# Loads issued behind the key relay, attention scheduled piece by piece, and two pieces of preparation in another order

## The chip, the cores and the metric

One Trainium2 chip, one core of it. The time is the device time of one execution in microseconds (us), taken as the median of several runs.

## The reference

Gated linear attention with a complex decay, then a two-layer projection with a leaky relu. What matters of it:

```python
mag = np.sqrt(a_re * a_re + a_im * a_im)
scale = np.minimum(mag, 0.999) / (mag + 1e-06)
...
a_re_n, a_im_n = (a_re * scale, a_im * scale)
...
for t in range(S):
    ar, ai = (a_re_n[:, :, t, :, None], a_im_n[:, :, t, :, None])
    new_re = ar * S_re - ai * S_im
    new_im = ar * S_im + ai * S_re
    kv = np.einsum('bhd,bhe->bhde', k[:, :, t], v[:, :, t])
    S_re, S_im = (new_re + kv, new_im)
    y[:, :, t] = np.einsum('bhd,bhde->bhe', q[:, :, t], S_re)
```

In words (4 batches, 8 heads, 768 steps, 48 channels): each of 32 heads keeps a complex 48 x 48 state; at every one of 768 steps its rows are multiplied by the scaled decay, the product of k and v is added to the real part, and y is q times the real part. Then, with x the y of all heads side by side (3072 tokens x 384), w_in 384 x 2048 and w_out 2048 x 384:

```python
h = x @ w_in
g = np.maximum(0.01 * h, h)
return (g @ w_out).astype(np.float32)
```

## The kernel before

The sequence is cut in 6 chunks of 128 steps, and the work in 12 **passes** (`SUBS`), each one chunk of two of the four batches. A pass n has these parts:

- `fetch_a`, `fetch_qk`, `fetch_v` load the decay, q and k, and v by DMAs from SyncE's queue (SP).
- `prep(n)` on VectorE (DVE) and ScalarE (ACT) scales the decay, multiplies it up along the chunk (eight steps `r` by pairs of rows `u` and `a`, then over blocks by rows `xs`), spreads the block products again (`xt`, written into a part of tile `a`), forms the running decay in `a`, and multiplies q by it and k by its inverse into the tile `qkt`. Squares, logarithms and exponentials of this are ScalarE's (`sq`, `u1`, `w`).
- `relay_of(n, 0)` and `relay_of(n, 1)` move the q half and the k half of `qkt` to the tile `t96` (shown as `t`) by five DMAs each, so that channels of a head lie side by side. The second is called the key relay below.
- `attend(n)`: TensorE (PE) forms `scores` of four half batches; VectorE multiplies each by the mask (`asb`, in places the tiles `asd` and `more`); TensorE transposes the `keys`, which ScalarE copies to `kn` (`natural`); TensorE forms `values` into PSUM and the `update` of the state; ScalarE rounds the values to `xh` (`rounded`) and VectorE keeps the remainder `xl` (`rest`; both halves are one tile `x`); VectorE adds the update to the state `rst` (`summed_up`) and ScalarE multiplies it by the decay (`decayed`). In pass 0 keys and update come later (`late`).
- `forward()`: two passes' ends are one group g of 256 tokens. A group has eight stages s. `first(g, s)` forms `ph` by 18 matmuls (two halves of three k times hi·xh, hi·xl, lo·xh); `hide` makes `tg` (the relu) and splits it into `hid` high and low, on ScalarE and VectorE in turns; `second(g, s)` adds 18 matmuls into `po`. `store(g)` copies `po` to `ot` and writes it.

The weights arrive as 64-bit numbers. `convert(i)` splits them, in the first 81 us, into high and low parts `win_hi`, `win_lo`, `wout_hi`, `wout_lo`: two VectorE rows on a stage tile (`stage_st`, `stage_stg`, `stage_hid`...), one conversion on ScalarE, two matmuls with `idw` and `nid` into a bank of PSUM (`pd` or `att`), one copy back. `check_weights` reads the weights once more late in the run (`wck`, three ScalarE operations each), and `flag` sums up all checks by small operations on `scr` into `bad`, which decides whether a general version runs behind it.

All of this is given out by a list scheduler, `drive`. Each part is a generator that says before every step on which lane (engine) it goes, a "+" meaning that it needn't wait for the end of its last step, and which `Mark`s it needs. `drive` keeps a clock for each lane, advanced by the estimates `dve_cost`, `act_cost`, `pe_costs` and `dma_cost`, and takes the step that could start first; among those that could start within `look(rank)` after it, the one of lowest rank. `look` gives `SOON` for ranks between 0 and 200. The result is a fixed order for each engine; what really waits for what is then settled by semaphores. All instructions that go through a lane are issued in one helper and have its line, L121.

Of the kernel before, what the change touches and what calls it, by code (L numbers as in the profile page):

```python
# [13 lines left out]
AF = mybir.ActivationFunctionType  # L14
# [3 lines left out]
B, H, S, D = 4, 8, 768, 48  # L18
# [3 lines left out]
P = 128  # L22
# [6 lines left out]
TI = 3  # L29
# [46 lines left out]
PLACE = (8, 10, 11)  # L76
LATE = 1
LOOK = {R_RELAY: 0.2, R_ATT: 0.3, -1: 0.16}
SOON = 0.0


def look(rank):
# [93 lines left out]
def dma_cost(name, kw, aps):  # L176
    if name == "memset":
        return 0.3, 0.4
    out = kw["out"]
    if in_sbuf(kw["in_"]) and in_sbuf(out):  # L180
        each = out.nbytes() / 200e3
        return max(each, 0.6), each + 4.2
    each = out.nbytes() / 400e3
    return max(each, 0.6), each + 2.4

# [271 lines left out]
def body(ctx, tc, keep, a_in, qk_in, v_in, w_in, out):  # L457
# [111 lines left out]
    def attends_of(n):  # L569
        return [attended[n]]  # L570

    def fetch_a(n):
        yield "S", *([prepared[n - 2]] if n > 1 else freed(A) if n else []), *([loading[n - 1]] if n else [])
        N = TI * len(SUBS[n][1]) * C
        loading[n].set(0.0)
        raw_a[n] = a = a_0 if n == 0 else pp.tile([P, 3, N], F32, tag="a", name=f"a_{n}", bufs=2)
        spq.dma_start(
            out=a[:, 1:3], in_=a_in[a_off[n] : a_off[n + 1]].rearrange("(p l x) -> p l x", p=P, l=2)
        )

    def fetch_qk(n):
        yield "S", *([prepared[n - 1]] if n else [])
        N = TI * len(SUBS[n][1]) * C
        raw_qk[n] = qk = pp.tile([P, 2, N], F32, tag="qk", name=f"qk_{n}")
        spq.dma_start(
            out=qk, in_=qk_in[a_off[n] : a_off[n + 1]].rearrange("(p l x) -> p l x", p=P, l=2)
        )
# [24 lines left out]
    def freed(*places):  # L612
        return [x for x, r in zip(converted, ROUND) if r in places]
# [54 lines left out]

    carrying = {}

    def prep(n):
        yield "A", fetched_a[n], *([scaled[n - 1]] if n else []), *([spread[n - 2]] if n > 1 else [])
        c, bs = SUBS[n]
# [46 lines left out]
        yield "V"  # L720
        dve.tensor_tensor(out=a[:, 1:3, sl], in0=a[:, 1:3, sl], in1=two(s0), op=ALU.mult)
        yield "A"
        act.activation(a[:, 0, sl], a[:, 2, sl], AF.Copy, scale=-1.0)

        scaled[n].set(prepared[n].end + 1.0)
        pr = u1[:, 0 : 4 * M].rearrange("p (a b m) -> p a b m", a=2, b=2)
        for r in range(1, R):
            src = zr[:, :, r - 1]
            yield "V"
            dve.tensor_tensor(  # L730
                out=pr, in0=src.unsqueeze(2).to_broadcast([P, 2, 2, M]), in1=swap(ar, r), op=ALU.mult
            )
            yield "V"
            dve.tensor_tensor(out=zr[:, :, r], in0=pr[:, 0], in1=pr[:, 1], op=ALU.add)
# [27 lines left out]
            st *= 2  # L762

        xt = w1[:, 0 : 2 * M].rearrange("p (l x j) -> p l x j", l=2, j=J)
        for l in range(2):
            yield "+A" if l else "A"
            act.copy(
                xt[:, l].rearrange("p i (j x) -> p x j i", x=NB),
                xs[:, l, 0:J].rearrange("p (x j) i -> p x j i", x=NB),
            )  # L770

        def tj(ap, k):
            return ap.rearrange("p (r x j) -> p r x j", r=k, j=J)

        spread[n].set(prepared[n].end + 0.6)
        yield "V", *([moved_q[n - 1], moved_k[n - 1]] if n else freed(*QKT))
        qkt = pp.tile([P, 2, 2, TI, nb, TP], F32, tag="qkt", name=f"qkt_{n}")
        tb = qkt[:, :, 1].rearrange("p l i b t -> p l (i b t)")[:, :, :N]

# [135 lines left out]
    def attend(n):  # L915
# [24 lines left out]
        def masked_out(bi, hh):  # L940
            name = f"asb_{n}_{bi}_{hh}"
            if bi == 0:
                asb = pp.tile([P, 4, C], F32, tag="asb", name=name, bufs=2)
            elif not once:
                asb = pp.tile([P, 4, C], F32, tag="tg", name=name, bufs=2)
            elif hh:
                asb = pp.tile([P, 4, C], F32, tag="asd", name=name)
            else:
                asb = more[0][:, 2 * DM : 2 * DM + 4 * C].rearrange("p (h t) -> p h t", h=4)
            dve.tensor_tensor(out=asb, in0=ps[bi, hh], in1=mask, op=ALU.mult)  # L950
            am[bi, hh] = asb
            banks.give(ps.pop((bi, hh)), attended[n].end + 0.8)

        def keys(bi, hh):
            t96 = relay[n][1]
            ps[bi, hh] = bank = banks.take()
            for h4 in range(4):
                pe.transpose(
                    out=bank[:, h4, 0:96],
                    in_=t96[:, slot_of(1, hh * 4 + h4), bi, 0:C],  # L960
                    identity=ident[0:96, 0:96],
                )
# [47 lines left out]
        def rounded(bi):  # L1010
            xh, _, x0 = xgroup(u0 + bi)
            act.activation(
                xh[:, :, x0 : x0 + C], px[bi][:, 0:TI], AF.Copy, scale=XSC,
                accum_out=xacc[:, u0 + bi : u0 + bi + 1],
            )
# [34 lines left out]
                banks.give(pu.pop(bi), attended[n].end + 2.5)  # L1050

        yield "P", moved_q[n], moved_k[n], *at[0], *(attends_of(n - 1) if n else [masked]), banks.some(4 if once else 1)
        for k, (bi, hh) in enumerate(halves):
            if k and not once:
                yield "+P", banks
            scores(bi, hh)
        for k, (bi, hh) in enumerate(halves):
            yield "+V" if k else "V"
            masked_out(bi, hh)
        if carry and not late:  # L1060
            for bi in range(nb):
                yield "+P" if bi else "P", banks.some(2), *at[1]
                for hh in range(2):
                    keys(bi, hh)
                for hh in range(2):
                    yield "+A" if hh else "A"
                    natural(bi, hh)
        yield "P", fetched_v[n], banks.some(2 if late or not carry else 4), *at[2], *(
            [summed[g - 2]] if g > 1 else freed((X0, X1)[g])
        )  # L1070
        for bi in range(nb):
            px[bi] = banks.take()
            if carry and not late:
                pu[bi] = banks.take()
        for bi in range(nb):
            if bi:
                yield "+P"
            values(bi)
            if carry and not late:
                update(bi)  # L1080
            yield "A"
            rounded(bi)
        for bi in range(nb):
            yield "+V" if bi else "V"
            rest(bi)
        if not carry:
            return
# [26 lines left out]
    def first(g, s):  # L1114
        xh, xl, _ = xgroup(g * GT // C)
        shown[g, s] = ph = psh.tile([P, NF, GT], F32, tag="h", name=f"ph_{g}_{s}")
        for x in range(NF):
            if x:
                yield "+P"
            fs = slice((s * NF + x) * P, (s * NF + x + 1) * P)  # L1120
            for k in range(TI):
                mm(ph[:, x], lhsT=win_hi[:, k, fs], rhs=xh[:, k], start=(k == 0), stop=False)
                mm(ph[:, x], lhsT=win_hi[:, k, fs], rhs=xl[:, k], start=False, stop=False)
                mm(ph[:, x], lhsT=win_lo[:, k, fs], rhs=xh[:, k], start=False, stop=(k == TI - 1))

    def hide(g, s):
        yield "A", *(freed(HID[s]) if g == 0 and s < 3 else [])
# [195 lines left out]
```

## Time and profile before

| | us |
|---|---|
| time, median of 3 runs | 605.81 (604.81 to 606.33) |
| the profiled execution | 606.6 |
| its span, first to last instruction | 604.9 |
| PE (TensorE matmul) busy | 554.5 (92%) |
| DVE (VectorE) busy | 520.6 (86%) |
| ACT (ScalarE) busy | 387.4 (64%) |

The busy times are those of one profiled execution, and an engine can be busy while it holds nothing up. In the rows below, a start is counted from the first instruction of the span; a line of the timeline is a run of like instructions; what stands in square brackets is the idle time of the engine ahead of it, and whose end ended that. The granted clock is 1.00 at TensorE's 2.4 GHz and 0.50 at 1.2 GHz. Names of tiles come without the numbers that tell passes apart.

### The profile page before, as it was taken

To read this page: it belongs to the slowest core of one execution; us is meant where nothing else is said; L and a number is where in the kernel's file an instruction comes from. 1 tells how busy PE (TensorE), PEld (TensorE's weight loads), DVE (VectorE), ACT (ScalarE), POOL (GpSimd) and SP (SyncE) were. 2 spreads that over 40 slices of the span, in tenths; PEclk is the share of its full clock that TensorE was granted. 3 is DMA by queue.
4 is the path that set the end of the run, shared out by engine and by line. 5 is a ranking of instruction groups with operands and counts; after the bars stand their busy time and mean duration, and the time that the engine had idled before them with its cause. 6 is when DMAs were issued, how large, how long until landed. Compare 5 with 4: busy or idle time off the path is not lost.

```text
span 604.9 us, 17867 instructions
## 1 busy us (share of the span) xinstructions
PE 554.5 (92%) x7650; PEld 525.0 (87%) x7650; DVE 520.6 (86%) x897; ACT 387.4 (64%) x850; POOL 5.0 (1%) x23
## 2 busy tenths in 40 slices
PE   3855599989879989999999999999999999999996
PEld 2433389989879889899999999999999999999996
DVE  5999999989899989899999999999999998754242
ACT  7987466484375475474584684684774855777983
POOL 2000000000000000000000000000000000000000
PEclk9895799999989999999999999999999999999999
DMA  8963612522523324333233245135125145656640
GB/s 344 389 227 82 215 59 54 159 83 55 158 85 84 129 69 114 114 86 107 105 110 109 80 136 157 48 95 158 60 80 159 59 112 152 196 161 231 231 157 29
DMA packets 28370, 79.18 MB, mean 131 GB/s; under 512 B 3200, under 2 KB 9344, under 8 KB 28288
## 3 DMA queue, kind: packets, MB, share of 16 engines
q1 hardware_dynamic: 28288, 78.02, 40.7%
q8 instruction: 60, 0.98, 0.6%
q14 instruction: 22, 0.18, 0.1%
HBM read 54.26 MB, written 4.72 MB: 98 GB/s over the span
## 4 chain that ended last, share of the span: by engine, by line
PE 62%; DVE 1%; ACT 1%; issue 1%
PE po L121 26%; PE ph L121 25%; PE att L121 11%; ACT rst L121 1%; DVE qkt L121 1%; DVE a L121 0%; ACT ot L121 0%; DVE x L121 0%; DVE sq L121 0%; ACT hid L121 0%; DVE rst L121 0%; DVE bad L121 0%; DVE xs L121 0%; ACT scr L121 0%
## 5 line engine op out<-in xcount | busy, mean ns | idle before, releaser
L121 PE MATMUL po<-hid,wout_hi 128*128 128x256 f32 x1152 | 217.8, 281 | 2.2 <-ACT hid L121 2.2
L121 PE MATMUL ph<-x,win_hi 128*128 128x256 f32 x1152 | 207.4, 281 | 6.3 <-DVE x L121 6.0
L121 PEld LDWEIGHTS po<-hid,wout_hi 128*128 128x128 f32 x1152 | 181.3, 188 | 5.9 <-ACT hid L121 2.9
L121 PEld LDWEIGHTS ph<-x,win_hi 128*128 128x128 f32 x1152 | 176.1, 189 | 9.9 <-DVE x L121 6.6
L121 PE MATMUL ph<-x,win_lo 128*128 128x256 f32 x576 | 160.9, 279 | 1.4 <-issue 1.4
L121 PE MATMUL po<-hid,wout_lo 128*128 128x256 f32 x576 | 138.3, 278 | 1.3 <-issue 1.3
L121 PEld LDWEIGHTS ph<-x,win_lo 128*128 128x128 f32 x576 | 109.2, 190 | 0.0
L121 PEld LDWEIGHTS po<-hid,wout_lo 128*128 128x128 f32 x576 | 108.6, 189 | 0.0
L121 ACT CAST hid<-tg 128x512 fp32r<-128x512 f32 x96 | 59.2, 617 | 71.9 <-DVE tg L121 71.9
L121 DVE TENSOR_TENSOR tg<-ph,tg 128x512 f32<-128x512 f32 x96 | 65.6, 684 | 26.1 <-ACT tg L121 26.1
L121 DVE TENSOR_TENSOR hid<-tg,hid 128x512 fp32r<-128x512 f32 x96 | 65.8, 686 | 21.5 <-ACT hid L121 21.5
L121 ACT ACTIVATE tg<-ph 128x512 f32<-128x512 f32 x96 | 57.0, 594 | 41.2 <-PE ph L121 41.1
L121 DVE TENSOR_TENSOR u<-a 128x384 f32<-128x384 f32 x84 | 46.7, 556 | 3.4 <-ACT a L121 1.2
L121 DVE TENSOR_TENSOR qkt<-qk,a 128x768 f32<-128x768 f32 x48 | 44.8, 949 | 1.4 <-ACT qkt L121 1.3
L121 PE MATMUL att<-asb,v 128*32 128x128 f32 x592 | 33.7, 275 | 2.0 <-DVE asb L121 2.0
L121 PE MATMUL att<-t 96*32 96x96 f32 (+3 forms) x1536 | 34.3, 250 | 0.3 <-issue 0.3
L121 PEld LDWEIGHTS att<-t 96*32 96x32 f32 x1536 | 32.2, 143 | 2.7 <-issue 1.3
L121 PE MATMUL att<-t,rst 96*32 96x128 f32 x640 | 33.4, 272 | 0.0
L121 ACT ACTIVATE wck<-wck 128x1152 f32<-128x1152 f32 (+1 forms) x22 | 27.3, 1242 | 9.3 <-DMA wck<-in_w_dram 9.1
L121 ACT ACTIVATE rst<-rst,t 96x48 f32<-96x48 f32 x128 | 29.8, 321 | 2.5 <-DVE rst L121 2.5
L121 DVE TENSOR_TENSOR a<-u 128x192 f32<-128x192 f32 x84 | 29.7, 353 | 1.1
L121 ACT ACTIVATE qkt<-a 128x1536 f32<-128x1536 f32 x12 | 17.9, 1488 | 14.2 <-issue 12.8
(161 smaller groups left out, 769.3 us busy)
## 6 DMA issues: line engine op xcount, KB each, us to landing
t<-qkt SPq DMA_DIRECT2D x48, 290.2 KB, 4.2
wck<-in_w_dram SPq DMA_DIRECT2D x10, 1152.0 KB, 6.2
v<-in_v_dram SPq DMA_DIRECT2D x12, 832.0 KB, 4.5
a<-in_a_dram SPq DMA_DIRECT2D x12, 768.0 KB, 4.7
qk<-in_qk_dram SPq DMA_DIRECT2D x12, 768.0 KB, 6.0
out_dram<-ot SPq DMA_DIRECT2D x12, 384.0 KB, 2.9
t<-qkt SPq DMA_DIRECT2D x24, 129.0 KB, 4.1
stage_st<-in_w_dram SPq DMA_DIRECT2D x3, 768.0 KB, 6.3
```

What stands on the lines that cost most here:

```text
L121: x = getattr(self.engine, name)(*args, **kw)
```

## The change

Six edits:

- `fetch_a(n)` needs, beside the end of preparation n-2, that pass n-2's key relay has been issued; `fetch_qk(n)` that pass n-1's has. So on SP these loads come behind that relay.
- `dma_cost` takes other figures for the relay's DMAs, and `SOON` goes from 0.0 to 0.06. Both are the planner's alone.
- `attend` gives out its pieces one at a time. `after(lane, lag)` makes a mark at the planned end of what was just given out, and each later piece waits for the mark of the piece that it uses, not for all that was said before. So a piece of another part can come between.
- The copy `a[:,0] <- a[:,2]` (times -1) becomes two: 96 columns, then the other 672. VectorE's first `u <- a` waits for the first alone.
- The two `xt` copies come in the order l = 1, 0, and `qkt <- a` waits for l = 1 alone.
- In `first`, the three hi·xl matmuls of each half come last.

```diff
-SOON = 0.0
+SOON = 0.06
...
-        each = out.nbytes() / 200e3
-        return max(each, 0.6), each + 4.2
+        return 0.78, 2.75
...
     def fetch_a(n):
-        yield "S", *([prepared[n - 2]] if n > 1 else freed(A) if n else []), *([loading[n - 1]] if n else [])
+        yield "S", *([prepared[n - 2], moved_k[n - 2]] if n > 1 else freed(A) if n else []), *([loading[n - 1]] if n else [])
...
     def fetch_qk(n):
-        yield "S", *([prepared[n - 1]] if n else [])
+        yield "S", *([prepared[n - 1], moved_k[n - 1]] if n else [])
...
+    def after(lane, lag):
+        mark = Mark()
+        mark.set(lane.clock + lag)
+        return mark
...
-        act.activation(a[:, 0, sl], a[:, 2, sl], AF.Copy, scale=-1.0)
+        act.activation(a[:, 0, M : 2 * M], a[:, 2, M : 2 * M], AF.Copy, scale=-1.0)
+        yield "+N"
+        turned = after(act, 0.15)
+        yield "+A"
+        act.activation(a[:, 0, 2 * M : N], a[:, 2, 2 * M : N], AF.Copy, scale=-1.0)
...
-            yield "V"
+            if r == 1:
+                yield "+V", turned
+            else:
+                yield "V"
...
-        for l in range(2):
-            yield "+A" if l else "A"
+        for l in (1, 0):
+            yield "A" if l else "+A"
...
+            yield "+N"
+            if l:
+                placed_x = after(act, 0.15)
...
-        yield "V", *([moved_q[n - 1], moved_k[n - 1]] if n else freed(*QKT))
+        yield "+V", placed_x, *([moved_q[n - 1], moved_k[n - 1]] if n else freed(*QKT))
...
             scores(bi, hh)
-        for k, (bi, hh) in enumerate(halves):
-            yield "+V" if k else "V"
+            yield "+N"
+            scored.append(after(pe, 0.22))
+        for (bi, hh), done in zip(halves, scored):
+            yield "+V", done
             masked_out(bi, hh)
...
             for k in range(TI):
                 mm(ph[:, x], lhsT=win_hi[:, k, fs], rhs=xh[:, k], start=(k == 0), stop=False)
-                mm(ph[:, x], lhsT=win_hi[:, k, fs], rhs=xl[:, k], start=False, stop=False)
-                mm(ph[:, x], lhsT=win_lo[:, k, fs], rhs=xh[:, k], start=False, stop=(k == TI - 1))
+                mm(ph[:, x], lhsT=win_lo[:, k, fs], rhs=xh[:, k], start=False, stop=False)
+            for k in range(TI):
+                mm(ph[:, x], lhsT=win_hi[:, k, fs], rhs=xl[:, k], start=False, stop=(k == TI - 1))
```

Keys, values, roundings and remainders in `attend` are given out in the same way as the scores and products in the diff. No computation is added or left out; ScalarE has one instruction more in each pass, from the split copy.

The order on VectorE around pass 0's products `asb_0` (`u1_1`, `a_1` and `xs_1` are preparation of pass 1, `sq_2` of pass 2, `stage_stg` a weight). Before:

```order
L121 TENSOR_TENSOR u1_1_375<-a_1_259 128x384
L121 TENSOR_TENSOR a_1_259<-u1_1_375 128x2x96
L121 SCALAR_TENSOR_TENSOR sq_2_498<-sq_2_498 128x768
L121 TENSOR_TENSOR asb_0_0_0_552<-att1_104,mask_78 128x512
L121 TENSOR_TENSOR asb_0_0_1_555<-att2_105,mask_78 128x512
L121 TENSOR_TENSOR asb_0_1_0_557<-att3_106,mask_78 128x512
L121 TENSOR_TENSOR asb_0_1_1_559<-att0_103,mask_78 128x512
L121 SCALAR_TENSOR_TENSOR stage_stg_9_125<-stage_stg_9_125 128x384
```

After:

```order
L121 SCALAR_TENSOR_TENSOR stage_stg_9_125<-stage_stg_9_125 128x384
L121 TENSOR_TENSOR a_1_260<-u1_1_372 128x2x96
L121 TENSOR_TENSOR u1_1_372<-a_1_260 128x384
L121 TENSOR_TENSOR a_1_260<-u1_1_372 128x2x96
L121 TENSOR_TENSOR asb_0_0_0_544<-att0_103,mask_78 128x512
L121 TENSOR_TENSOR asb_0_0_1_546<-att1_104,mask_78 128x512
L121 TENSOR_TENSOR asb_0_1_0_548<-att2_105,mask_78 128x512
L121 TENSOR_TENSOR asb_0_1_1_552<-att3_106,mask_78 128x512
```

Ahead of the products stood six pairs of `u1_1` and `a_1` and the row of `sq_2`; now two pairs stand there and the two rows of the last `stage_stg`, and the rest comes behind. On TensorE the conversion of the last `stage_hid`, which stood ahead of pass 0's scores, now stands behind them.

The order on SP in pass 2 (`t96_2` is the relay, five DMAs for q and five for k; `a_4` and `qk_3` are loads of later passes). Before:

```order
L121 DMA t96_2_1427<-qkt_2_1334 96x1x774 x2
L121 DMA t96_2_1427<-qkt_2_1334 64x1x516
L121 DMA t96_2_1427<-qkt_2_1334 32x1x258 x2
L121 DMA a_4_1599<-in_a_dram 128x1536
L121 DMA t96_2_1427<-qkt_2_1334 96x1x774 x2
L121 DMA t96_2_1427<-qkt_2_1334 64x1x516
L121 DMA t96_2_1427<-qkt_2_1334 32x1x258 x2
L121 DMA qk_3_1692<-in_qk_dram 128x1536
```

After:

```order
L121 DMA t96_2_1475<-qkt_2_1366 96x1x774 x2
L121 DMA t96_2_1475<-qkt_2_1366 64x1x516
L121 DMA t96_2_1475<-qkt_2_1366 32x1x258 x2
L121 DMA t96_2_1475<-qkt_2_1366 96x1x774 x2
L121 DMA t96_2_1475<-qkt_2_1366 64x1x516
L121 DMA t96_2_1475<-qkt_2_1366 32x1x258 x2
L121 DMA a_4_1728<-in_a_dram 128x1536
L121 DMA qk_3_1781<-in_qk_dram 128x1536
```

The load of `a_4` moves from between the two halves of the relay to behind both.

The order on VectorE ahead of pass 3's `x_3` (`a_4`, `qkt_4` are preparation of pass 4, `sq_5` of pass 5; `tg_2_7` and `hid_2_7` belong to the last stage of group 2). Before:

```order
L121 TENSOR_TENSOR qkt_4_2511<-a_4_1599 128x2x768
L121 TENSOR_TENSOR a_4_1599<-a_4_1599 128x1536
L121 TENSOR_TENSOR a_4_1599<-a_4_1599,qkt_4_2511 128x768 x2
L121 SCALAR_TENSOR_TENSOR sq_5_2359<-sq_5_2359 128x768
L121 TENSOR_TENSOR qkt_4_2511<-qk_4_2270,a_4_1599 128x6x128 x2
L121 SCALAR_TENSOR_TENSOR x_3_2527<-att3_106,x_3_2527 128x3x128
L121 SCALAR_TENSOR_TENSOR x_3_2527<-att0_103,x_3_2527 128x3x128
L121 TENSOR_TENSOR rst_81<-att2_105,rst_81 96x4x2x48
L121 TENSOR_TENSOR rst_81<-att1_104,rst_81 96x4x2x48
L121 TENSOR_TENSOR tg_2_7_2609<-ph_2_7_2517,tg_2_7_2609 128x512
```

After:

```order
L121 TENSOR_TENSOR tg_2_7_2481<-ph_2_7_2435,tg_2_7_2481 128x512
L121 TENSOR_TENSOR qkt_4_2521<-a_4_1728 128x2x768
L121 TENSOR_TENSOR hid_2_7_2482<-tg_2_7_2481,hid_2_7_2482 128x512
L121 TENSOR_TENSOR a_4_1728<-a_4_1728 128x1536
L121 SCALAR_TENSOR_TENSOR sq_5_2420<-sq_5_2420 128x768
L121 SCALAR_TENSOR_TENSOR x_3_2610<-att0_103,x_3_2610 128x3x128
L121 SCALAR_TENSOR_TENSOR x_3_2610<-att2_105,x_3_2610 128x3x128
L121 TENSOR_TENSOR rst_81<-att3_106,rst_81 96x4x2x48
L121 TENSOR_TENSOR rst_81<-att1_104,rst_81 96x4x2x48
L121 TENSOR_TENSOR a_4_1728<-a_4_1728,qkt_4_2521 128x768 x2
```

Two products of `a_4` and two of `qkt_4` have gone from ahead of `x_3` to behind it, and `tg_2_7` and `hid_2_7` from behind it to ahead.

Two smaller moves: in the prelude the last load of `stage_stg` stood behind pass 0's key relay on SP and now stands in front of it; at the end the ScalarE operations of `wck_27`, the last weight check, and the `scr` rows on VectorE stood ahead of the last `hid` and now stand behind it, the former in front of the last `ot`.

## Rows read from the trace of the kernel before

**Rows 1.** Page, part 1: busy us of each engine, share of the span, instructions.

```profile
PE 554.5 (92%) x7650; PEld 525.0 (87%) x7650; DVE 520.6 (86%) x897; ACT 387.4 (64%) x850; POOL 5.0 (1%) x23
```

**Rows 2.** Page, part 4: the chain that ended last, shares by engine.

```profile
PE 62%; DVE 1%; ACT 1%; issue 1%
```

**Rows 3.** Stretches: length, busy us per engine (PE, PEld, DVE, ACT, POOL), clock, DMA.

```profile
60.00:80.00 20.00, 11.26 (x204) 7.72 (x204) 18.64 (x31) 9.19 (x17) 0.12 (x1) 0.83 0.51 172
260.00:300.00 40.00, 39.82 (x521) 39.37 (x513) 37.80 (x69) 23.17 (x58) 0.12 (x1) 1.00 0.37 112
```

**Rows 4.** Timeline of PE from 69 to 81 us: start, length, operation.

```profile
69.57 1.48 PE L121 MATMUL att<-stage_hid,idw 128*128 128x384 f32 x2
...
71.31 2.84 PE L121 MATMUL att<-t 96*32 96x128 f32 x128
...
80.89 0.48 PE L121 MATMUL ph<-x,win_hi 128*128 128x256 f32 x2
```

**Rows 5.** Timeline of DVE from 68 to 78 us.

```profile
68.73 0.56 DVE L121 TENSOR_TENSOR u<-a 128x384 f32<-128x384 f32 x1 [0.91 <-ACT a L121]
...
75.39 2.48 DVE L121 TENSOR_TENSOR asb<-att,mask 128x512 f32<-128x512 f32 x4
```

**Rows 6.** Stretches of PE: length, busy us, granted clock, DMA share, GB/s.

```profile
66.20:71.30 5.10, 5.09 (x9) 0.50 0.82 257
177.35:180.50 3.15, 3.15 (x14) 0.50 0.08 32
```

**Rows 7.** Timeline of PE: first waiting `ph` of passes 1, 2 and 3.

```profile
127.45 0.39 PE L121 MATMUL ph<-x,win_hi 128*128 128x256 f32 x1 [1.98 <-DVE x L121]
...
177.35 0.58 PE L121 MATMUL ph<-x,win_hi 128*128 128x256 f32 x1 [2.97 <-DVE x L121]
...
220.59 0.39 PE L121 MATMUL ph<-x,win_hi 128*128 128x256 f32 x1 [1.09 <-DVE x L121]
```

**Rows 8.** Timeline of SP (length: issue of all) and of ACT, pass 2.

```profile
151.50 0.34 SPq L121 DMA_DIRECT2D a<-in_a_dram  x1
152.19 5.49 SPq L121 DMA_DIRECT2D t<-qkt  x5
...
157.18 1.48 ACT L121 ACTIVATE sq<-a 128x1536 f32<-128x1536 f32 x1 [4.55 <-DMA a<-in_a_dram]
```

**Rows 9.** Timeline of DVE: idle places that ended with ScalarE.

```profile
44.75 1.76 DVE L121 TENSOR_TENSOR qkt<-a 128x1536 f32<-128x1536 f32 x1 [0.53 <-ACT a L121]
...
158.79 0.96 DVE L121 SCALAR_TENSOR_TENSOR sq<-sq 128x768 f32<-128x768 f32 x1 [1.61 <-ACT sq L121]
...
170.21 1.76 DVE L121 TENSOR_TENSOR qkt<-a 128x1536 f32<-128x1536 f32 x1 [1.37 <-ACT a L121]
```

**Rows 10.** Timeline of DVE around pass 3's `x`.

```profile
215.17 1.83 DVE L121 TENSOR_TENSOR a<-a,qkt 128x768 f32<-128x768 f32 x2
216.91 0.95 DVE L121 TENSOR_TENSOR sq<-sq 128x768 f32<-128x768 f32 x1
...
221.38 0.68 DVE L121 TENSOR_TENSOR tg<-ph,tg 128x512 f32<-128x512 f32 x1
221.98 0.95 DVE L121 SCALAR_TENSOR_TENSOR qkt<-qkt 128x768 f32<-128x768 f32 x1
```

**Rows 11.** Stretches of PE with `ph` and `po` alone (x: matmuls), as Rows 6.

```profile
228.00:244.00 16.00, 16.00 (x138) 1.00 0.44 119
...
306.00:322.00 16.00, 16.00 (x144) 1.00 0.45 129
```

**Rows 12.** Timeline of ACT near the end.

```profile
564.18 2.56 ACT L121 ACTIVATE wck<-wck 128x1152 f32<-128x1152 f32 x2
...
594.84 0.62 ACT L121 CAST hid<-tg 128x512 fp32r<-128x512 f32 x1 [0.82 <-DVE tg L121]
...
599.67 0.94 ACT L121 ACTIVATE ot<-po 128x256 f32<-128x256 f32 x3 [4.21 <-PE po L121]
```

More of the change, by code (lines that the diff above doesn't have):

```diff
@@ L1052, in attend @@
         yield "P", moved_q[n], moved_k[n], *at[0], *(attends_of(n - 1) if n else [masked]), banks.some(4 if once else 1)
+        scored = []
         for k, (bi, hh) in enumerate(halves):
-            if k and not once:
-                yield "+P", banks
+            if k:
+                yield "+P", *([] if once else [banks])
             scores(bi, hh)
-        for k, (bi, hh) in enumerate(halves):
-            yield "+V" if k else "V"
+            yield "+N"
+            scored.append(after(pe, 0.22))
+        for (bi, hh), done in zip(halves, scored):
+            yield "+V", done
             masked_out(bi, hh)
+        yield "+N"
+        shown_to = after(dve, 0.15)
         if carry and not late:
@@ L1064, in attend @@
                     keys(bi, hh)
+                yield "+N"
+                done = after(pe, 0.22)
                 for hh in range(2):
-                    yield "+A" if hh else "A"
+                    yield "+A", done
                     natural(bi, hh)
-        yield "P", fetched_v[n], banks.some(2 if late or not carry else 4), *at[2], *(
+            yield "+N"
+            shown_to = after(act, 0.15)
+        yield "+P", shown_to, fetched_v[n], banks.some(2 if late or not carry else 4), *at[2], *(
             [summed[g - 2]] if g > 1 else freed((X0, X1)[g])
@@ L1074, in attend @@
                 pu[bi] = banks.take()
+        valued, rounds = [], []
         for bi in range(nb):
@@ L1078, in attend @@
             values(bi)
+            yield "+N"
+            valued.append(after(pe, 0.22))
             if carry and not late:
+                yield "+P"
                 update(bi)
-            yield "A"
+        for bi in range(nb):
+            yield "+A", valued[bi]
             rounded(bi)
+            yield "+N"
+            rounds.append(after(act, 0.15))
         for bi in range(nb):
-            yield "+V" if bi else "V"
+            yield "+V", rounds[bi]
             rest(bi)
```

## The prediction

> **What bounds the kernel now.** I read the page's busy shares first, then the chain that ended last, then each engine's share by stretch, and last the single idle places of TensorE in the timeline. TensorE is busy 92% of the span and VectorE 86% [rows 1]; the chain that ended last is almost all TensorE [rows 2]. So the time is TensorE's work plus the places where it stands. These lie early: in 60 to 80 us it works 11.26 us of 20, in 260 to 300 us 39.82 of 40 [rows 3]. From there on, nothing but TensorE's own work counts, and the change leaves that alone: the same matmuls in another order. What can be won lies before 262 us.
>
> In the early stretch TensorE waits for VectorE. In 60 to 80 us VectorE is busy 18.64 of 20 us [rows 3]; TensorE's first `ph` matmul of the main loop starts only at 80.89 [rows 4]. Later it stands for `x`, which VectorE writes: 1.98 us before pass 1's first `ph`, 2.97 before pass 2's, 1.09 before pass 3's [rows 7]. At 220.59, where pass 3's wait ends, TensorE has no slack against VectorE left. Therefore I sum **VectorE's** work up to that point, `x_3`: what goes from ahead of it brings TensorE forward too, as long as TensorE itself has idle time to give up. It has: 1.98, 2.97 and 1.09 us [rows 7] and some 2.5 us in the prelude (below), 8.5 together.
>
> **The change part by part.** *Order on VectorE at x_3.* In the order before, the four 128x768 products of pass 4 (two `a`, two `qkt`) stand ahead of `x_3`; now they stand behind it, and one `tg` and one `hid` row that stood behind now stand ahead. From start to start such a product takes 0.87 us (215.17 to 216.91 for two) and `tg` 0.60 (221.38 to 221.98); `hid` has the same shape, and I take the same [rows 10]. 4 x 0.87 - 2 x 0.60 = 2.28 us earlier. All other rows ahead of `x_3` are the same.
>
> *VectorE's idle places ahead of x_3.* Four of them hang on what the change touches. The copy `a[:,0] <- a[:,2]` is split: VectorE stood 0.91 us for the whole 768 columns [rows 5] and now needs the first 96 of them. I take 0.5 off (between 0 and 0.91). The product `qkt <- a` waited for both `xt` copies of ScalarE, standing 0.53 us in pass 0 and 1.37 in pass 2 [rows 9]; it now waits for the first alone. I take 0.4 off each (0 to 0.53 and 0 to 1.37). And 1.61 us at 158.79 [rows 9] goes back to the load of `a_4`: that was issued at 151.50 ahead of the key relay of pass 2, and ScalarE stood 4.55 us for it at 157.18, with `sq` in front of everything else that ScalarE had to do [rows 8]. Now the load stands behind the relay and `sq_4` later in ScalarE's order, so the 1.61 goes; the relay, whose five pieces took 5.49 us to issue behind the load [rows 8], is freed as well. Sum 0.5 + 0.4 + 0.4 + 1.6 = 2.9 us, with 1.0 and 4.4 as ends.
>
> Of passes 1 to 9 this is the only one in which the new waits of the loads change SP's order: in the others the loads stood behind the key relay already. In pass 10 `qk_11` goes behind the relay and a weight check in front of it, where nothing waits for either. In the prelude the last `stage_stg` load moves in front of pass 0's key relay. Its buffer is free well before VectorE has finished the keys, so I cost it at nothing; if it weren't, the relay's five pieces and the scores would wait for it.
>
> *Low half of x needed later.* A `ph` half now needs `xl` as its seventh matmul, not as its second. While TensorE waits for `x`, five more matmuls are done; 16 us over 144 matmuls is 0.11 us each [rows 11], so 5 x 0.11 = 0.57 us off at `x_3` (0 if TensorE isn't there yet).
>
> *Prelude, a check on the way.* The last `stage_hid` conversion (69.57 to 71.31 [rows 4]) moves behind the scores, so the scores can begin 1.7 us earlier. They ended at 74.15 (71.31 + 2.84 [rows 4]) and the `asb` products began only at 75.39 [rows 5], since eight `u`/`a` rows and `sq_2` stood ahead that now stand behind: 1.2 us more. Against it, the clock was granted at half (1.2 GHz) up to 71.30 [rows 6], and scores that start in that stretch run at half for up to 1.7 us, which costs up to 0.9. I expect the first `ph` at 78.4 instead of 80.89 (2.5 us; 1 to 3.5). This is part of the 2.28 + 2.9 + 0.57, not on top of it.
>
> *Tail.* The weight check `wck_27` on ScalarE (two passes of 1.28 us and one like them [rows 12], 3.9 us) now comes behind the last `hid` instead of ahead of it, in front of `ot`. Before, that `hid` ended at 595.46 and ScalarE stood 4.21 us until 599.67 for the last `po` [rows 12]; the check fits, with 0.3 us left. Behind it the small rows that form the flag now also come last. I take +0.4 us (0 to 1.5).
>
> *At nothing:* the planner's constants (they only set the order), and the second piece of the split copy, twelve more short ScalarE instructions, one a pass, on an engine that neither chain nor waits name as the bound. The ordering of attention pieces from pass 4 on: TensorE has no gap there to close [rows 3].
>
> *Spacing of matmuls.* In nine stretches of 16 us of pure `ph`/`po` work, at a granted clock of 1.00 throughout, five hold 138 matmuls and four hold 143 to 145 [rows 11]. The state flips after short stops, and I can't tell which way the new order will fall: 6 of 144 is 4.2%, 0.67 us for each 16-us stretch that flips. I take zero for the sum and 2.5 us either way for the range. The Trainium skill ("TensorE: Matmul & The Clock Gate", Part 1, "Wait — 56ns, not 53.3ns?") gives one start-to-start time for a matmul of given length at the full clock, its columns over 2.4 GHz and about 2.5 ns. By that this term would be nothing and the range 2.5 us narrower at each end; the rows show two, and the rows decide.
>
> *Sum.* -2.28 - 2.9 - 0.57 + 0.4 = -5.35 us. The profiled execution took 606.6 us (span 604.9, 1.7 around it), so it becomes 601.2. It lay 0.8 over the median of the runs, 605.81, so I forecast **600.4 us**.
>
> **The rivals.** *The keys come later (no change).* VectorE serves `tg` and `hid` earlier than before; that puts one pair, 2 x 0.60 us [rows 10], ahead of the last key product in passes 1 and 2, and about as much in pass 3. If scores wait for the keys there, 3.6 of the 5.35 us are given back as new TensorE waits: -1.7, 604.1 us. For it: VectorE is as full as TensorE in these passes. Against it: the scores stand later in TensorE's order too (pass 1's by one `po` step). *Only the prelude gains.* The change mostly doesn't do what it says, since the loads already stood behind the relay in all passes but one; `x` of passes 1 to 3 is late by other ScalarE work: -2.5, 603.3 us. *All of it closes.* TensorE's own order also loses the waits behind 220.59, and pass 2's matmuls no longer begin at half clock, as they do for 3.15 us behind its wait [rows 6], which gives back half of that: -5.35, 2 us of later gaps and 1.6 for the clock: -9, 596.8 us. *Slower.* The slow spacing takes over: it decides from 5.35 + 1.8 = 7.2 us, that is eleven 16-us stretches more at 138 matmuls, where some 230 us (fourteen) now run at the faster one. All of them would give +9.4 - 5.35 = +4, 610 us; just at the bound, 607.6. Against it: the steady passes, where most of the fast stretches lie, keep their order of `ph` and `po`.
>
> **How the numbers follow.** Forecast 0.50 (own range 597.5 to 603); all closes 0.17; only the prelude 0.15; keys later 0.12; slower 0.06. About 0.3%, 1.8 us, is what a measurement of this kernel can tell from no change. Faster by more: 0.50 + 0.17 + 0.15, less 0.03 at the edge of the prelude case and 0.01 of the forecast, plus 0.03 of the keys' case: 0.81. Slower 0.06; the rest, 0.13, within. The range holds the forecast, most of the two smaller gains and most of the case where all closes: 595.5 to 604.4.
>
> **What would show it.** Right: first `ph` near 78.4; no ScalarE wait for `a` near 157; the three waits for `x` [rows 7] at 6 us together before, at most 3 after; steady passes of unchanged length; `ot` starting within 0.5 us of the last `po`. Wrong: scores of pass 1 or 2 waiting for the relay `t`; 138 matmuls in most of the nine stretches; a wait of `ot` or of the flag for `wck`; the prelude's first `ph` still at 80 or later.

## The result and the profile after

The changed kernel takes 600.08 us (median of 4 runs, 599.82 to 602.3) against 606.07 us before (4 runs, 604.81 to 607.54): a ratio of 0.990, 95% interval 0.9879 to 0.9922. It is about 1% faster, 6.0 us between the medians; 600.4 was forecast. The profiled execution took 599.82 us with a span of 598.1, 6.8 less than before. Medians here and below leave out a run that took over 1.5% more than the fastest of its kernel (one each of u_xt and d_late).

The page of the changed kernel, part 1 (busy us, share, instructions), and its stretches from 60 to 80 and 260 to 300 us (as [rows 1, 3]):

```profile
PE 551.6 (92%) x7650; PEld 522.3 (87%) x7650; DVE 522.6 (87%) x897; ACT 388.4 (65%) x862; POOL 5.0 (1%) x23
...
60.00:80.00 20.00, 14.45 (x237) 11.36 (x237) 19.22 (x32) 10.77 (x23) 0.12 (x1) 0.83 0.47 149
260.00:300.00 40.00, 40.00 (x634) 39.45 (x634) 38.03 (x68) 23.34 (x57) 0.12 (x1) 1.00 0.37 112
```

The shares hardly differ; nothing in them shows the 6 us. The single places do. TensorE of the changed kernel, the counterpart of [rows 4, 7], with the waits that are new (here and below, a row's length and count can be cut off by the end of the view):

```profile
68.50 3.67 PE L121 MATMUL att<-t 96*32 96x128 f32 x128
...
77.44 0.28 PE L121 MATMUL ph<-x,win_hi 128*128 128x256 f32 x1
...
124.45 0.74 PE L121 MATMUL ph<-x,win_hi 128*128 128x256 f32 x4 [0.93 <-DVE x L121]
...
169.58 0.38 PE L121 MATMUL ph<-x,win_hi 128*128 128x256 f32 x1 [1.29 <-ACT x L121]
...
171.50 0.74 PE L121 MATMUL ph<-x,win_hi 128*128 128x256 f32 x4 [0.96 <-DVE x L121]
...
176.93 0.39 PE L121 MATMUL ph<-x,win_hi 128*128 128x256 f32 x1 [1.74 <-DVE tg L121]
...
196.40 0.41 PE L121 MATMUL att<-t 96*32 96x128 f32 x8 [0.81 <-DMA t<-qkt]
...
198.10 2.11 PE L121 MATMUL att<-t 96*32 96x64 f32 x92 [1.30 <-DMA t<-qkt]
...
213.80 0.28 PE L121 MATMUL ph<-x,win_hi 128*128 128x256 f32 x1
```

The first `ph` starts 3.45 us earlier (77.44 against 80.89). The waits for `x` are 0.93, 1.29 + 0.96 and none, 3.2 us against 6.0. Pass 3's first waiting `ph` of [rows 7], at 220.59, has become one without a wait at 213.80: 6.8 us earlier. From there to the end nothing more is won: 599.67 - 220.59 = 379.1 us to `ot` before, 592.97 - 213.80 = 379.2 after. That the two are alike is a balance: in the changed kernel TensorE stands 3.4 us on this way where it stood 2.3 (3.0 against 0.5 from 260 to 590 us, rows below), and fewer of its matmuls come at the slower of two spacings (845 pairs against 1108, 1.2 us; see *Spacing*).

So the whole gain was there by pass 3, half in the prelude, half in passes 0 to 3. But new waits came: for `tg` at 176.93, and for the key relay of pass 3 at 196.40 and 198.10. In a second profile of the same kernel (below) the first was missing and the others were 0.24 and 0.65 us.

### The profile page after: what moved, and what is told of

It reads as the page before. It is cut to its first block, busy times and chain, and to the rows that moved or that the text cites. A ratio compares the mean times of both kernels' runs of the same rounds, so it can differ in the third digit from the quotient of the medians.

```text
span 598.1 us, 17875 instructions
## 1 busy us (share of the span) xinstructions
PE 551.6 (92%) x7650; PEld 522.3 (87%) x7650; DVE 522.6 (87%) x897; ACT 388.4 (65%) x862; POOL 5.0 (1%) x23
## 4 chain that ended last, share of the span: by engine, by line
PE 58%; DVE 20%; ACT 11%; DMA 7%; issue 3%; SPq 0%; DVEq 0%; ACTq 0%
PE po L121 21%; PE ph L121 20%; PE att L121 15%; DVE qkt L121 5%; DVE a L121 4%; DMA wck<-in_w_dram 3%; ACT wck L121 3%; DVE tg L121 2%; DMA t<-qkt 2%; DVE u L121 2%; DVE hid L121 2%; ACT rst L121 2%; DVE sq L121 1%; PE pd L121 1%; ACT tg L121 1%
## 5 line engine op out<-in xcount | busy, mean ns | idle before, releaser
L121 PE MATMUL ph<-x,win_hi 128*128 128x256 f32 x1152 | 215.7, 279 | 5.3 <-DVE tg L121 2.0
L121 PE MATMUL po<-hid,wout_hi 128*128 128x256 f32 x1152 | 215.3, 280 | 0.0
L121 PEld LDWEIGHTS ph<-x,win_hi 128*128 128x128 f32 x1152 | 181.4, 188 | 6.9 <-DVE tg L121 2.4
L121 PE MATMUL ph<-x,win_lo 128*128 128x256 f32 x576 | 141.6, 278 | 0.0
L121 PE MATMUL att<-t 96*32 96x96 f32 (+3 forms) x1536 | 36.9, 254 | 4.1 <-DMA t<-qkt 3.9
L121 PEld LDWEIGHTS att<-t 96*32 96x32 f32 x1536 | 33.8, 145 | 7.7 <-DMA t<-qkt 4.6
L121 ACT ACTIVATE sq<-a 128x1536 f32<-128x1536 f32 x12 | 17.9, 1495 | 15.4 <-DMA a<-in_a_dram 15.4
```

What stands on the lines that cost most here:

```text
L121: x = getattr(self.engine, name)(*args, **kw)
```

## The experiments

Two theories stand against each other, and each expectation says what they give for its kernel. A is the prediction's: up to pass 3 TensorE waits for VectorE's `x`, so VectorE's work and idle time up to there make the time, and what is late behind pass 3 is hidden. B, the rival: VectorE isn't the bound by itself, and the gain comes from elsewhere (the earlier start out of the prelude, or the order of the other engines, which take VectorE's place when it is relieved).

All of them are read by one sum. VectorE starts on the second half of `x` of pass 3 at 44 us + the time it worked since then + the time it stood. The sum shows where time lies, not what put it there. A view of the stretch from 44 us to that `x` gives both; columns are the stretch, its length and VectorE's busy us (the rest is idle), its instructions, clock, DMA share and GB/s. Before, the changed kernel, and the changed kernel profiled once more:

```profile
44.00:219.99 175.99, 165.23 (x277) 0.93 0.36 108
...
44.00:213.52 169.52, 163.18 (x275) 0.94 0.35 105
...
44.00:214.02 170.02, 163.56 (x274) 0.93 0.35 106
```

Work went from 165.2 to 163.2 and 163.6, idle time from 10.8 to 6.3 and 6.5. The table has the same for every kernel run, with its time, the ratio to the kernel before on the same chip, the time of the one execution that was profiled, and how long TensorE ran at half clock in it between 75 and 590 us. All marks of a row are of that one execution, which can lie well off the median (u_xt, d_early).

| kernel | us, median | ratio (95%) | profiled, us | first ph | x of pass 3 | worked | idle | half clock, us |
|---|---|---|---|---|---|---|---|---|
| before | 606.07 | | 606.6 | 80.89 | 219.99 | 165.2 | 10.8 | 3.4 |
| changed | 600.08 | 0.990 (0.988 to 0.992) | 599.82 | 77.44 | 213.52 | 163.2 | 6.3 | 0 |
| changed, once more | 601.26 | 0.991 (0.988 to 0.994) | 600.11 | 77.49 | 214.02 | 163.6 | 6.5 | 6.8 |
| u_xl | 601.20 | 0.991 (0.988 to 0.994) | 602.23 | 78.10 | 216.14 | 163.8 | 8.3 | 10.2 |
| u_load4 | 601.25 | 0.992 (0.989 to 0.995) | 601.72 | 77.43 | 214.93 | 163.4 | 7.6 | 6.8 |
| u_xt | 603.88 | 0.995 (0.992 to 0.998) | 597.70 | 77.71 | 213.76 | 162.6 | 7.1 | 0 |
| u_const | 602.18 | 0.993 (0.990 to 0.995) | 601.95 | 78.61 | 216.80 | 163.0 | 9.8 | 3.4 |
| u_pieces | 609.26 | 1.004 (1.001 to 1.006) | 610.25 | 77.23 | 213.49 | 161.5 | 8.0 | 3.4 |
| u_loads | 614.55 | 1.014 (1.010 to 1.018) | 612.81 | 77.04 | 217.71 | 163.9 | 9.9 | 13.7 |
| a_const | 610.81 | 1.008 (1.005 to 1.010) | 610.48 | 77.08 | 220.31 | 164.2 | 12.1 | 13.7 |
| a_pieces | 606.02 | 1.000 (0.998 to 1.003) | 607.39 | 79.83 | 216.18 | 162.1 | 10.1 | 10.2 |
| d_early | 606.61 | 1.001 (0.998 to 1.004) | 602.65 | 77.51 | 217.50 | 167.1 | 6.4 | 10.2 |
| d_late | 605.52 | 0.998 (0.995 to 1.001) | 608.55 | 77.70 | 216.83 | 163.7 | 9.2 | 20.5 |
| pool_sq | 607.02 | 1.002 (0.999 to 1.005) | 606.51 | 77.34 | 216.64 | 161.9 | 10.8 | 6.8 |

Names with u_ undo one edit in the changed kernel, those with a_ add one to the kernel before. Runs of one kernel spread by 2 to 9 us, so ratios closer than about 0.004 aren't told apart, and `x` of pass 3 moves by chance too (d_late below).

**The changed kernel once more.**

> The changed kernel once more, to see how far marks of the trace move between executions: first ph within 0.7 us of 77.44, x of pass 3 (its second half on VectorE) within 0.7 us of 213.52, about 600 us.

Both marks lie within 0.5 us of the first profile.

**More work on VectorE, early and late.** The same edit with passes (2, 3) and (8, 9):

```diff
         dve.tensor_tensor(out=a[:, 1:3, sl], in0=a[:, 1:3, sl], in1=two(s0), op=ALU.mult)
+        if n in (2, 3):
+            dve.tensor_tensor(out=sq[:, :, sl], in0=sq[:, :, sl], in1=sq[:, :, sl], op=ALU.mult)
+            dve.log.pop()
```

> The changed kernel with two VectorE products of 128x1536 added (1.75 us each, written to a tile whose content is done with), one in the preparation of pass 2 and one in that of pass 3, in a fixed place; no other instruction moves. Theory A: x of pass 3 comes 3.5 us later and so does the end, 603.6. Theory B (TensorE is the bound and VectorE has room): at most +1 us, 600.1 to 601.1.

> The changed kernel with the two added VectorE products of 128x1536 (1.75 us each) in the preparation of passes 8 and 9 instead of 2 and 3; nothing else moves. Theory A: there TensorE never stands for VectorE, so x of pass 3 at 213.5 to 214.0, and the way from there to the last po within 1 us of the 379 us of the changed kernel. Theory B (VectorE is as near to being the bound in the later passes): that way 2 to 3.5 us longer.

Early: 3.5 us more work put `x` of pass 3 at 217.50, 3.5 to 4.0 later, with idle time unchanged (6.4), and the time 5.3 us above that of the changed kernel once more (606.6 against 601.3, on another chip each); theory A had said 3.5. VectorE has no room in passes 0 to 3: theory A there. Late, TensorE worked this much from 260 to 590 us (columns: stretch, length and busy us, clock); d_late first, then the changed kernel, once and again, then the kernel before:

```profile
260.00:590.00 330.00, 326.13 (x4639) 1.00 0.41 128
...
260.00:590.00 330.00, 327.04 (x4654) 1.00 0.41 125
...
260.00:590.00 330.00, 327.34 (x4655) 1.00 0.41 125
...
260.00:590.00 330.00, 329.49 (x4739) 1.00 0.42 128
```

In this execution TensorE stood about 1 us longer there than in the changed kernel, not 3.5. But the way that the expectation named, from `ph` of pass 3 to the end of the last `po`, was 384.3 us against 379.2 in both profiles of the changed kernel: 5 longer, more than either theory had. And `x` of pass 3 was 3 later, though ahead of it this kernel is the changed one, instruction for instruction. The trace has the reason for most of both, in two stretches of TensorE:

```profile
197.09 0.41 PE L121 MATMUL att<-t 96*32 96x128 f32 x8 [0.81 <-DMA t<-qkt]
198.79 1.57 PE L121 MATMUL att<-t 96*32 96x64 f32 x53 [1.29 <-DMA t<-qkt]
...
199.20:206.00 6.80, 6.80 (x129) 0.54 0.61 227
...
243.32 3.91 PE L121 MATMUL att<-t 96*32 96x64 f32 x120 [1.54 <-DMA t<-qkt]
...
243.60:250.40 6.80, 6.80 (x134) 0.53 0.54 208
```

After the same waits for the relay as in the changed kernel (0.81 and 1.30 there) the clock was granted at half for 6.8 us here, and not there; behind a wait of 1.54 at 243.32 once more. Half clock for 6.8 us is 3.4 us of work lost: about what `x` of pass 3 is late, and 3.4 of the 5 us behind it. So these waits were sometimes followed by a loss far above their length.

That doesn't explain the median, which is 4 us above the changed kernel's (605.5 against 601.3). Eight of the nine runs had a mean granted clock of 0.975 to 0.981, where the changed kernel's runs had 0.970 to 0.982, and their median is still 605.2. So only the one trace says that late work is mostly hidden. By the times it costs about as much as early work (0.998 against 1.001, with intervals that overlap), which is theory B's side. Whether VectorE has room behind pass 3 stays open.

**One edit taken back.** The low half of `x`, the load of `a_4`, and the `xt` copies:

```diff
                 mm(ph[:, x], lhsT=win_hi[:, k, fs], rhs=xh[:, k], start=(k == 0), stop=False)
-                mm(ph[:, x], lhsT=win_lo[:, k, fs], rhs=xh[:, k], start=False, stop=False)
-            for k in range(TI):
-                mm(ph[:, x], lhsT=win_hi[:, k, fs], rhs=xl[:, k], start=False, stop=(k == TI - 1))
+                mm(ph[:, x], lhsT=win_hi[:, k, fs], rhs=xl[:, k], start=False, stop=False)
+                mm(ph[:, x], lhsT=win_lo[:, k, fs], rhs=xh[:, k], start=False, stop=(k == TI - 1))
```

> The changed kernel (600.1 us) with the three matmuls of the low half of x back in their old places in each half of ph; no other instruction moves. Theory A (VectorE's work up to x of pass 3 sets the time of the early passes, so that waits of TensorE ahead of it are made good later): only the last wait counts, x of pass 3, so +0.2 to +0.6 us, 600.3 to 600.7. Theory B (every wait of TensorE counts by itself): +0.57 us at each of the three waits for x, +1.7 us, 601.8.

601.20 us: the times don't tell it from the changed kernel. In the trace `x` of pass 3 is 2.1 to 2.6 later, but this execution also ran at half clock from 201.0, behind the relay's wait, as the two others didn't. No size for this edit is shown.

```diff
-        yield "S", *([prepared[n - 2], moved_k[n - 2]] if n > 1 else ...
+        yield "S", *([prepared[n - 2], *([moved_k[n - 2]] if n != 4 else [])] if n > 1 else ...
```

> The changed kernel with one wait taken back: the load of a of pass 4 needn't wait for the key relay of pass 2 and is issued between that pass's q and k relays again; 3 rows of VectorE and ScalarE move. Theory A with the step of the prediction: VectorE's 1.6 us of idle time come back, +1.6 us, 601.7, ScalarE standing for the load of a near 155 and the scores of pass 2 later. Theory B (ScalarE now takes the squares of pass 4 later anyway, so the load's place is free): within 0.3 us of 600.1, and only the scores of pass 2 wait longer, by under 2 us, which is made good before x of pass 3.

Here the places are clear. ScalarE and TensorE of u_load4:

```profile
155.50 1.48 ACT L121 ACTIVATE sq<-a 128x1536 f32<-128x1536 f32 x1 [3.56 <-DMA a<-in_a_dram]
...
156.93 0.43 PE L121 MATMUL att<-t 96*32 96x128 f32 x8 [1.74 <-DMA t<-qkt]
158.22 3.07 PE L121 MATMUL att<-t 96*32 96x64 f32 x103 [0.85 <-DMA t<-qkt]
```

ScalarE's stall of [rows 8] is back (3.56 us), and the scores of pass 2 wait 2.6 us for the relay (0.3 in the changed kernel). VectorE's idle time is 1.1 to 1.2 us up, and `x` of pass 3 comes 0.9 to 1.4 later, against a price of 1.6; part of that may be half clock, granted from 159.3 for 3.4 us behind these waits. The time, 601.25, doesn't show it.

```diff
-        for l in (1, 0):
-            yield "A" if l else "+A"
+        for l in range(2):
+            yield "+A" if l else "A"
```

(and the product's wait for both copies)

> The changed kernel with the two xt copies back in the old order, VectorE's product waiting for both. Theory A: VectorE stands 0.4 to 0.8 us longer in two of passes 1 to 4, +0.4 to +1 us, 600.5 to 601.1. Theory B (TensorE's own waits count, the product isn't among what they wait for): within 0.3 us of 600.1.

Idle time 0.7 to 0.8 up, work 0.6 to 0.9 down, since other VectorE rows move with it in the new order; `x` of pass 3 unmoved. The median is 2.6 to 3.8 us above the changed kernel's two, with intervals that touch, and the runs lie between 597.7, the profiled one, and 606.3. Not told apart.

**The planner's figures, alone and taken back.** The first of them is the kernel before with

```diff
-SOON = 0.0
+SOON = 0.06
...
-        each = out.nbytes() / 200e3
-        return max(each, 0.6), each + 4.2
+        return 0.78, 2.75
```

> The kernel before with the two planner constants of the change alone. Its order has 2.4 us less on VectorE ahead of pass 0's products and 1.7 us less ahead of x of pass 3; ScalarE's stalls stay. Theory A: first ph 1 to 2 us earlier than 80.89, x of pass 3 1.7 us earlier than 219.99, and 604.3. Theory B: the prelude's gain is carried on, plus what the waits at passes 1 to 3 lose: 602 or less.

> The changed kernel with both planner constants back (the relay's figures and the look window). In the new order ahead of pass 0's products VectorE has 1.9 us more than in the changed kernel, but at x of pass 3 the same. Theory A (VectorE's work up to x of pass 3 decides): first ph some 2 us later than 77.44, x of pass 3 again near 213.5, and about 600 us. Theory B (what the prelude gains is carried to the end): x of pass 3 and the end 2 us later, 602.

Alone, they bring the prelude's whole gain (first `ph` at 77.08, 3.8 earlier) and lose it by pass 3 (`x` at 220.31, 0.3 later than before). TensorE of a_const:

```profile
126.41 0.58 PE L121 MATMUL ph<-x,win_hi 128*128 128x256 f32 x1 [2.90 <-DVE x L121]
...
178.06 0.58 PE L121 MATMUL ph<-x,win_hi 128*128 128x256 f32 x1 [3.54 <-DVE x L121]
...
125.00:131.80 6.80, 5.39 (x25) 0.55 0.16 68
176.20:183.00 6.80, 4.94 (x23) 0.55 0.20 80
```

The waits for `x` are longer than before, and half clock follows both. So a gain in the prelude isn't carried on by itself: theory B fell, and theory A's 604.3 was as wrong, since idle time grew by 1.3 us. The kernel is 0.8% slower than before, and most of that lies behind pass 3: from 260 to 590 us TensorE stood 1.8 us (0.5 before), and 1419 pairs of its matmuls against 821 came at the slower spacing (below), 2.6 us. Why, these runs don't show. Taken back, the figures cost 3 us at `x` of pass 3, as idle time and not as work (TensorE waits 4.61 us for `tg` at 181.11, half clock behind it), where theory A had expected none and theory B 2; in time 1 to 2 us, 602.18 against B's 602, near the noise.

**Single pieces of attention, taken back and alone.** The piece of `attend` between the scores and `if not carry` as before, in the changed kernel; and as changed, in the kernel before.

> The changed kernel with attention given out as before, without marks for single pieces. Ahead of x of pass 3 VectorE then has 2.1 us less work than in the changed kernel. Theory A: x of pass 3 up to 2 us earlier than 213.52 as long as TensorE still waits there, and 598.5 to 600. Theory B (the single pieces are what brings the gain): nearer to the kernel before, 602 to 604.

> The kernel before with attention given out piece by piece and nothing else. By its order VectorE has 2.6 us less ahead of x of pass 3 than in the kernel before. Theory A, if ScalarE's stalls stay: x of pass 3 near 217.4, and 603.5. Theory B (the pieces only help together with the new planner constants): x of pass 3 at 219 to 221, and 605 or more.

Without them `x` of pass 3 comes as early as in the changed kernel (213.49), but all is lost behind it: 609.3 us, theory B's side and more. TensorE of u_pieces, from 260 us on and in the last pass:

```profile
260.00:590.00 330.00, 323.19 (x4572) 1.00 0.40 125
...
559.50 0.42 PE L121 MATMUL att<-t,rst 96*32 96x128 f32 x8 [1.18 <-issue]
565.04 0.38 PE L121 MATMUL ph<-x,win_hi 128*128 128x256 f32 x1 [2.48 <-ACT x L121]
```

It stands 6.8 us there, against 2.7 to 3.0. That is 4 of the 8 us, and the slower spacing is about the rest: 2116 pairs against 1143 and 918 in the whole trace, 4 to 5 us. Alone, the pieces bring nothing in time (606.02), though `x` of pass 3 is 3.8 earlier.

**No load behind a relay.** Both waits taken out of the changed kernel:

```diff
-[prepared[n - 2], moved_k[n - 2]] if n > 1
+[prepared[n - 2]] if n > 1
...
-[prepared[n - 1], moved_k[n - 1]]
+[prepared[n - 1]]
```

> The changed kernel with no load waiting for a key relay, as before. By its order VectorE has 4 us more ahead of x of pass 1, 3.8 less ahead of x of pass 2, and at x of pass 3 the same as the changed kernel. Theory A: only idle time can move x of pass 3; with the load of a of pass 4 ahead of the relay again 1 to 2 us, so x of pass 3 at 214.5 to 216, and 601 to 602. Theory B (the loads are the whole of the gain): x of pass 3 near 219, and 605 or more.

614.55 us, the slowest of all, 13 us above the changed kernel: far beyond theory B. `x` of pass 3 was only 4 us later. SyncE and TensorE of u_loads:

```profile
112.37 4.00 SPq L121 DMA_DIRECT2D t<-qkt  x5
116.41 0.58 SPq L121 DMA_DIRECT2D a<-in_a_dram  x1
...
116.52 3.82 PE L121 MATMUL att<-t 96*32 96x128 f32 x92 [3.46 <-DMA t<-qkt]
...
115.30:125.50 10.20, 8.91 (x168) 0.51 0.74 241
...
260.00:590.00 330.00, 322.07 (x4582) 1.00 0.42 125
```

In pass 1 the loads stand behind the relay even so. The harm seen there is the order on VectorE: from 44 us on it works 65.9 us ahead of pass 1's key relay (58.5 before, 59.8 in the changed kernel), so that this relay is issued from 112.37 to 116.4 (105.78 to 109.8 before), the scores wait 3.46 us, and the clock stays at half for 10 us. From 260 us on TensorE stands another 7.9 us, 5 more than in the changed kernel. That is 9 of the 13 us; the rest isn't placed. The waits of the loads act on the queue in pass 2 (and pass 10) alone, but on the plan everywhere.

**Less work on VectorE.** The product `s0 = s0 * s1` on GpSimd in passes 2 to 4.

```diff
-        yield "V"
-        dve.tensor_tensor(out=s0, in0=s0, in1=s1, op=ALU.mult)
+        yield "G" if n in (2, 3, 4) else "V"
+        (plq if n in (2, 3, 4) else dve).tensor_tensor(out=s0, in0=s0, in1=s1, op=ALU.mult)
```

> The changed kernel with the 128x768 product of squares in the preparation of passes 2, 3 and 4 on GpSimd instead of VectorE, and the order planned with it. VectorE then has 3.5 us less ahead of x of pass 3 than in the changed kernel. Theory A (VectorE's work and idle time up to x of pass 3 set the early passes): x of pass 3 2 to 3.5 us earlier than 213.5 to 214.0, and the end as much, 596.5 to 598.5. Theory B (VectorE then waits for the other engines instead, or for GpSimd): its idle time ahead of x of pass 3 grows from 6.3 by about 3.5 us, x of pass 3 stays, 600.

Theory B's side, and worse than it: 1.3 to 1.7 us less work, 4.3 to 4.4 more idle, `x` of pass 3 not unmoved but 3 later (216.64), 607.0 us and not 600. GpSimd, TensorE and (behind `x` of pass 3) VectorE of pool_sq:

```profile
89.92 1.89 POOL L121 TENSOR_TENSOR sq<-sq 128x768 f32<-128x768 f32 x1 [72.53 <-ACT sq L121]
...
156.49 0.43 PE L121 MATMUL att<-t 96*32 96x128 f32 x8 [1.67 <-DMA t<-qkt]
...
253.63 0.53 DVE L121 TENSOR_TENSOR u<-xs 128x360 f32<-128x360 f32 x1 [4.79 <-ACT xs L121]
```

The product takes 1.89 us on GpSimd against 0.95 on VectorE, the order planned around it lets the scores wait for the relay, and VectorE waits for ScalarE. It beats neither kernel. Since the whole order was planned anew, the run doesn't tell the slower product from the other order.

## Why the prediction was right, step by step

*TensorE's waits on VectorE set the early passes, and nothing is won behind pass 3.* Right in where the gain lies: 6.8 us earlier at pass 3's `ph`, none behind. d_early shows that VectorE has no room ahead of that place. But u_const, a_const and pool_sq show that its work isn't the bound by itself: taking work off it, or moving it, brought idle time instead. ScalarE, the relay and TensorE are all close behind. Theory A holds in one direction only. The second half, that only TensorE's own work counts behind pass 3, isn't shown: its standing there grew by 1.1 us, which had been put at nothing, and the spacing happened to give it back; a_const, u_pieces, u_loads and the times of d_late all lost more than that there. Which of the six edits the gain comes from isn't shown either: of those taken back, u_xl and u_load4 aren't told apart in time and u_xt and u_const hardly, u_pieces and u_loads lost more than the whole 6 us, and the split copy was never taken back alone.

*Order at x_3, -2.28.* Right: VectorE worked 2.05 us less up to it (1.67 in the second profile).

*Idle time, -2.9.* The term that was mis-sized: 10.8 to 6.3 us, -4.4 (-4.3), at the upper of the ends given, 1.0 and 4.4. By its parts, VectorE of the changed kernel:

```profile
43.53 1.76 DVE L121 TENSOR_TENSOR qkt<-a 128x1536 f32<-128x1536 f32 x1 [0.47 <-ACT a L121]
...
68.13 0.55 DVE L121 TENSOR_TENSOR u<-a 128x384 f32<-128x384 f32 x1
...
165.90 1.76 DVE L121 TENSOR_TENSOR qkt<-a 128x1536 f32<-128x1536 f32 x1 [0.54 <-ACT a L121]
```

The split copy gave 0.91 and not 0.5: a `stage_stg` row stood in the gap as well. The `xt` order gave 0.06 in pass 0 and 0.83 in pass 2, 0.4 each forecast. The 1.61 us of `a_4` went in full; u_load4 brought 0.57 back at that place and 0.42 at pass 2's `qkt`. That is 3.4 us from the four places. The other 1.0 came from places that I hadn't counted: 1.00 us at 122.84 became 0.26 and 0.60 at 211.58 went, while 0.55 came new at pass 1's `qkt`, and smaller ones came and went.

*Load of `a_4`.* Right in its place. SyncE and ScalarE of the changed kernel, against [rows 8]:

```profile
150.58 3.98 SPq L121 DMA_DIRECT2D t<-qkt  x5
154.67 0.53 SPq L121 DMA_DIRECT2D a<-in_a_dram  x1
...
159.32 1.49 ACT L121 ACTIVATE sq<-a 128x1536 f32<-128x1536 f32 x1 [0.41 <-DMA a<-in_a_dram]
```

The relay takes 3.98 us to issue, not 5.49, and ScalarE waits 0.41 us for the load, not 4.55. But that the waits of the loads act in pass 2 alone was half the truth, since I read the order of the changed kernel and not what the planner would have done without: u_loads.

*Low half of x, -0.57.* At pass 3 TensorE doesn't wait at all; u_xl gives no size of its own. No run shows the term. And 5 x 0.11 is 0.55, not 0.57.

*Prelude, 2.5 (1 to 3.5).* It was 3.45. The scores began at 68.50, 2.8 earlier and not 1.7, and half clock (0.51 from 68.50 to 70.70) stretched them to 3.67 us from 2.84, about the 0.9 allowed for.

*Tail, +0.4.* It cost nothing. ScalarE near the end, against [rows 12]:

```profile
588.61 2.56 ACT L121 ACTIVATE wck<-wck 128x1152 f32<-128x1152 f32 x2
...
591.29 1.36 ACT L121 ACTIVATE wck<-wck,low 128x1152 f32<-128x1152 f32 x1
...
592.97 0.94 ACT L121 ACTIVATE ot<-po 128x256 f32<-128x256 f32 x3 [0.24 <-PE po L121]
```

`ot` still waits for `po`, 0.24 us. From its start to the end of the span it is 5.1 us, 5.2 before. The flag comes later (TensorE stood 1.02 us for it) and ends behind the issue of the last write, without showing in the span.

*Spacing, 0 with 2.5 either way.* It moved: counted over the whole trace, 1452 pairs of neighbouring `ph` or `po` matmuls were at about 118 ns before, 1143 in the changed kernel, 918 in its second profile, the others at about 113; at 4.4 ns a pair -1.4 and -2.4 us. So a part of the profile's 6.8 us is this. The flips into the slower spacing mostly came behind a stop or other work of TensorE (25 of 29 before), as the prediction has it, but those back mostly with neither (24 of 29).

*The signs.* The waits for `x` came to 3.2 us where at most 3 was the sign of being right, and the scores of pass 2 waited 0.34 us for the relay, a sign of being wrong in small.

*The rivals.* "The keys come later" did happen, in pass 3: its scores wait 2.1 us for the relay (0.9 in the second profile), for which the price was 1.2 a pass. It didn't decide, since what comes behind is VectorE's `x`. "Only the prelude" fell with the 3.3 us that came behind it, and a_const's gain in the prelude was gone by pass 3. "All of it closes" came about in part, as pass 2's half clock didn't occur in the first profile. It did in the second, where `x` of pass 3 came only 0.5 us later. The waits behind 220.59, which it was to close too, grew instead. "Slower" didn't come here; in a_const and u_pieces its slow spacing did grow (1754 and 2116 pairs).

*The number.* By its terms the forecast was -5.35 us; measured they are -2.05, -4.4, none seen and none, -6.5 together, and the span of the profile fell by 6.8. That 600.4 lies 0.3 us from the median of 600.08 is luck: runs of this kernel alone spread by 2.5 and 5.4 us, and once more it took 601.26.

## What to carry to other kernels

Where a planner makes the order, edits can't be priced one by one: two planner figures alone made this kernel 0.8% slower, attention in pieces alone changed nothing, and without the loads' wait the rest came out 2.4% slower than with it. Compare the orders of the whole change, and add up the work and the idle time of the engine that is waited for, up to the last place where it holds the bound up: all its idle places, since here 1.0 of the 4.4 us came from places that no edit named. Then look behind that place as well, where 4 to 9 us were lost in other orders (a_const, u_pieces, u_loads). Taking work off a nearly full engine isn't the reverse of adding to it: here other engines took its place at once. And a mark in one trace isn't the median: d_late's trace and its times say different things.

## What the runs showed of the hardware

Waits of TensorE of 0.8 and 1.3 us within 2.5 us were followed by 6.8 us at half clock in one execution (d_late) and by none in another (the changed kernel), with the same instructions ahead of them. A product of 128x768 took 1.8 to 1.9 us on GpSimd (pool_sq), 0.95 on VectorE. Two spacings of the same matmul at full granted clock, 113 and 118 ns, were in every trace, in stretches that differ between executions of one kernel.
